# New places for row sums, loads and second-MLP units in an attention-plus-MLP kernel on one core

## The chip, the core and the metric

One core of one Trainium2 chip. The metric is the device time of one execution in microseconds, the median of several; less is better. A time from the timed runs is some 1.8 us longer than the span of the profile of the same execution, and I keep the two apart.

## The reference

```python
# q, k, v: (8, 12, 448, 64) fp32; w_in (768, 2048), w_out (2048, 768)
q_n, k_n = rmsnorm(q, g_q), rmsnorm(k, g_k)          # over the last dim
scores = q_n @ k_n.T / 8
attn = softmax(scores)
x = (attn @ v) -> (3584, 768)
h = x @ w_in
g = maximum(h, 0) + alpha * minimum(h, 0)            # alpha per column, 0 to 0.3
out = g @ w_out                                      # (3584, 768) fp32
```

## The kernel before

A *group* y is four heads of one batch (24 groups, three to a batch). Its q and k are loaded, squared, summed by row, turned into 1/rms (the *root*, two small ACT instructions), scaled, transposed by TensorE and copied out of PSUM as qT and kT. The score tiles follow two at a time; I call what is emitted between two pairs of them a *stretch* (index n). A stretch may hold the denominators ("dn"), the values ("av") or the transposes ("tps") of a group, and in it stand units of the MLP of an earlier batch: u (first MLP, 6 matmuls) and D (second MLP, 16 matmuls). `square`, `reduce`, `root` and `scale` prepare a group:

```python
    def square(y, nm):
        src = nat[y, nm].rearrange("p h j d -> p (h j d)")
        sq = ld.tile([128, 2 * J, D], FP32, name="sq", tag="sq", bufs=2)
        sqf = sq.rearrange("p n d -> p (n d)")
        if y < 2:
            nc.scalar.activation(out=sqf, in_=src, func=AF.Square)
        else:
            nc.gpsimd.tensor_mul(out=sqf, in0=src, in1=src)
        sqs[y, nm] = sq

    def reduce(y, nm):
        if nm == "q":
            ss_t[y] = ld.tile([128, 2, 2, J], FP32, name="ss", tag="ss", bufs=4)
        nc.vector.tensor_reduce(
            out=ss_t[y][:, "qk".index(nm)].rearrange("p h j -> p (h j)").unsqueeze(2),
            in_=sqs[y, nm], axis=AXIS_X, op=ALU.add,
        )
# ... root: two ACT instructions on ss -> rr; scale: tensor_mul by rr on POOL, for three tiles on DVE
    def turn(y):

        ps = psa.tile([128, 2, 512], FP32, name="tps", tag="acc")
# ...  14 transposes into ps, then on DVE:
        for tp, nm in zip(tps, "qk"):
            t = att.tile([128, 2, J, 64], FP16, name=f"{nm}T", tag=f"{nm}T", bufs=3)
            o = t.rearrange("p g j c -> p j g c")
            i4 = tp.rearrange("p j (g c) -> p j g c", g=2)
            if nm == "q":
                nc.vector.tensor_copy(out=o, in_=i4)
            else:
                nc.vector.tensor_scalar(
                    out=o, in0=i4, scalar1=gain[:, 0:1], scalar2=None, op0=ALU.mult
                )
            qkT[y, nm] = t
```

The two kinds of units share two PSUM buffers (tag "mm"). A first-MLP unit's result leaves PSUM by an ACT copy and a DVE max, a second-MLP unit's by a DVE copy:

```python
    def up(b, ft):
        x = xT[b].rearrange("p g i c -> p (g i) c")
        hT = psf.tile([128, 512], FP32, name="hT", tag="mm")
        for c in range(KM):
            nc.tensor.matmul(
                out=hT[:, :S],
                lhsT=w_in_sb[:, c, ts(ft, 128)],
                rhs=x[:, c, :],
                start=(c == 0),
                stop=(c == KM - 1),
            )
        ah = ffn.tile([128, S], FP16, name="ah", tag="ah", bufs=3)
        nc.scalar.activation(out=ah, in_=hT[:, :S], func=AF.Copy, scale=alpha_sb[:, ft : ft + 1])
        nc.vector.tensor_max(out=gT[:, ft, ds((b & 1) * S, S)], in0=hT[:, :S], in1=ah)

    def down(b0, t, oh):

        op = psf.tile([128, 512], FP32, name="op", tag="mm")
        for ft in range(NF):
            nc.tensor.matmul(
                out=op[:, :OH],
                lhsT=gT[:, ft, ts(t, 128)],
                rhs=w_out_sb[:, ft, ds(oh * OH, OH)],
                start=(ft == 0),
                stop=(ft == NF - 1),
            )
        if oh == 0:
            osb[b0, t] = ffn.tile([128, DM], FP32, name="osb", tag="osb", bufs=3)
        o = osb[b0, t]
        nc.vector.tensor_copy(out=o[:, ds(oh * OH, OH)], in_=op[:, :OH])
        if oh == 1:
            for half in range(2):
                bb, j = divmod(2 * t + half, J)
                nc.sync.dma_start(out=out4[b0 + bb, j], in_=o[ds(64 * half, 64)])
```

Where things are emitted, and the loop (cut):

```python
    for y in range(G, NG):
        n = J * y / 2
        at(n - 12, load_qk, y)
        for nm in "qk":
            at(n - 6, square, y, nm)
            after(n - 5, reduce, y, nm)
        after(n - 4, root, y)
        for nm in "qk":
            at(n - 3, scale, y, nm)
    for b in range(1, B):
        at(J * G * b / 2 - 4, load_v, b)
    turns = {J * y // 2 - 1: y for y in range(1, NG)}
# ... merge() spreads the carried D evenly among a batch's 16 u; half of the new D stay in the period
    after(0, root, 1)
    for nm in "qk":
        after(0, scale, 1, nm)
        after(1, reduce, 2, nm)
    after(2, root, 2)
    for nm in "qk":
        after(2, scale, 2, nm)

    for n in range(NB + 2):
        for f, a in prep.get(n, ()):
            f(*a)
        tiles = [divmod(m, J) for m in (2 * n, 2 * n + 1) if m < NG * J]
        for t in tiles:
            score(*t)
        late = []
        if n in dens:
            den(dens[n])
        if n in avs:
            attv(avs[n])
        plain = n not in dens and n not in avs and n not in turns
        wait = plain and gaps[n] and gaps[n][0][0] is up
        for t in tiles[:1] if wait else tiles:
            soft(*t)
        if wait:
            late = [(soft, t) for t in tiles[1:]]
        if n in dens:
            log(dens[n])
            late = [(invert, (dens[n],))]
        if n in turns:
            turn(turns[n])
        for f, a in gaps[n]:
            f(*a)
            if f is up and late:
                for g, c in late:
                    g(*c)
                late = []
        for g, c in late:
            g(*c)
        if n < first:
            spin(1 if not plain else 4)
        for f, a in post.get(n, ()):
            f(*a)
    for f, a in rest:
        f(*a)

```

The softmax here doesn't subtract the row's maximum and nothing guards it: scores larger than these inputs give would overflow.

## Time and profile before

| | before |
|---|---|
| timed runs | 490.51 us median (489.69 to 491.06, 4 runs) |
| profiled run | 488.3 us, span 486.5 us |
| first MLP unit starts | 51.92 us |
| listed waits of TensorE, 53 to 434 us | 15.5 us for DVE's max, 0.8 for DVE's multiply |

The profiled run is faster than each of the four timed ones. The lines of this profile are shown in the prediction below: the busy line, the table by stages, the waits of TensorE, the timeline of one large wait, and the start.

From the matmul records I took the start of each unit minus the start of the unit before it, and subtracted the smallest such difference of the same pair of kinds in this profile, for every kernel the same (1.133 us from u to u, 1.225 from u to scores, 2.597 from D to u, 0.505 from scores to transposes, and so on). The sum from the first u to the end is what TensorE lost; I call it *start-to-start loss*. Before: 24.55 us. The listed 0.25 is a loss of 0.41 in this measure, 1.02 is 1.18, 1.36 is 1.52: the list counts from the modelled end of the unit before, and that end lies some 0.16 us after the moment at which the next unit can start (a u is shown 1.29 to 1.30 long and followed by the next after 1.133).

### The profile page before, as it was taken

How to read it: one execution, taken by the hardware profiler on the slowest of the kernel's cores; microseconds unless marked ns; L12 is line 12 of the kernel's file. 1: busy time of each engine (PE TensorE's matmuls, PEld its weight loads, DVE VectorE, ACT ScalarE, POOL GpSimd, SP SyncE). 2: the span in 40 equal slices, each digit the busy share in tenths (PEclk: the TensorE clock that was granted, in tenths of full speed). 3: DMA queues.
4: the chain of work that ended last, by engine and by line, in shares of the span. 5: the costliest groups of instructions: out<-in, count | busy, mean ns of one | idle time of the engine just before them, and what ended most of it. 6: DMA issues, size and time to landing. Idle time of an engine off the chain costs nothing.

```text
span 486.5 us, 9510 instructions
## 1 busy us (share of the span) xinstructions
PE 448.4 (92%) x4072; PEld 234.3 (48%) x4072; DVE 216.7 (45%) x312; ACT 290.7 (60%) x399; POOL 166.7 (34%) x123
## 2 busy tenths in 40 slices
PE   6768799999999899999999899999999899999995
PEld 2334354544555444554555454554555454454563
DVE  1753545453552454544562444634643542334421
ACT  2688788666754667557765656666776475523300
POOL 2767574606504425405415244423435020000000
PEclk9599999999999999999999999999999999999999
DMA  7999996343605081333532280333511110120122
GB/s 210 158 248 244 239 197 117 71 109 87 134 23 124 20 165 51 91 98 85 96 74 74 70 166 5 105 80 97 100 34 34 34 34 0 34 66 0 34 65 66
DMA packets 32187, 45.46 MB, mean 93 GB/s; under 512 B 5008, under 2 KB 28560, under 8 KB 32144
## 3 DMA queue, kind: packets, MB, share of 16 engines
q1 hardware_dynamic: 19504, 31.67, 25.5%
q0 software_dynamic: 11776, 11.80, 15.3%
q10 hardware_dynamic: 864, 1.38, 1.0%
q8 instruction: 32, 0.52, 0.4%
q14 instruction: 11, 0.09, 0.1%
HBM read 45.62 MB, written 11.01 MB: 116 GB/s over the span
## 4 chain that ended last, share of the span: by engine, by line
PE 71%; DVE 13%; ACT 11%; DMA 2%; issue 2%; POOL 0%; DVEq 0%
PE op L266 31%; PE hT L249 20%; PE sc L189 6%; PE dn L212 6%; DVE ss L133 5%; DVE gT L258 5%; ACT ah L257 5%; PE av L212 5%; ACT expT L201 4%; PE tps L166 3%; DMA nat<-in_q_dram 2%; ACT rden L232 1%; DVE kT L176 1%; DVE qT L174 1%; ACT rden L227 1%
## 5 line engine op out<-in xcount | busy, mean ns | idle before, releaser
L201 ACT ACTIVATE expT<-sc,expb 128x896 f16<-128x896 f32 x168 | 160.2, 1003 | 48.7 <-PE sc L189 48.4
L249 PE MATMUL hT<-xT,w_in_sb 128*128 128x448 f16 x768 | 159.5, 352 | 17.9 <-DVE gT L258 17.0
L266 PE MATMUL op<-w_out_sb,gT 128*128 128x384 f16 x896 | 152.9, 326 | 0.2 <-DVE gT L258 0.2
L150 POOL TENSOR_TENSOR qs<-nat,rr 128x896 f16<-128x896 f32 x45 | 75.0, 1686 | 221.6 <-ACT rr L145 211.8
L257 ACT ACTIVATE ah<-hT,alpha_sb 128x448 f16<-128x448 f32 x128 | 81.1, 634 | 101.7 <-PE hT L249 100.7
L258 DVE TENSOR_TENSOR gT<-hT,ah 128x448 f16<-128x448 f32 x128 | 79.5, 624 | 104.3 <-ACT ah L257 104.2
L249 PEld LDWEIGHTS <-w_in_sb 128*128 128x128 f16 x768 | 72.3, 97 | 95.0 <-issue 35.4
L266 PEld LDWEIGHTS <-gT 128*128 128x128 f16 x896 | 85.0, 98 | 64.1 <-issue 10.5
L276 DVE COPY osb<-op 128x384 f32<-128x384 f32 x56 | 31.2, 558 | 112.1 <-PE op L266 112.1
L127 POOL TENSOR_TENSOR sq<-nat 128x896 f32<-128x896 f32 x44 | 72.9, 1676 | 3.0 <-DVE ss L133 3.0
L189 PE MATMUL sc<-qT,kT 64*64 64x448 f16 x672 | 50.2, 367 | 7.5 <-DVE kT L176 5.8
L133 DVE TENSOR_REDUCE ss<-sq 128x14 f32<-128x896 f32 x48 | 49.7, 1076 | 9.1 <-ACT sq L125 9.1
L240 DVE TENSOR_TENSOR xT<-av,rden 128x896 f16<-128x896 f32 x24 | 26.2, 1091 | 31.6 <-PE av L212 31.6
L212 PE MATMUL av<-expT,vt 64*64 64x448 f16 x672 | 36.0, 349 | 1.2 <-ACT rden L227 1.2
L212 PE MATMUL dn<-expT,ones 64*64 64x448 f16 x672 | 35.9, 349 | 0.0
L189 PEld LDWEIGHTS <-kT 64*64 64x64 f16 x672 | 13.4, 105 | 38.6 <-issue 30.2
L166 PE MATMUL tps<-ident,qs 128*128 128x128 f16 x336 | 24.0, 224 | 4.7 <-POOL qs L150 4.4
L212 PEld LDWEIGHTS <-vt 64*64 64x64 f16 x672 | 20.0, 107 | 13.5 <-issue 2.3
L166 PEld LDWEIGHTS <-qs 128*128 128x128 f16 x336 | 19.4, 100 | 13.5 <-issue 7.0
L212 PEld LDWEIGHTS <-ones 64*64 64x64 f16 x672 | 19.9, 107 | 11.8 <-issue 0.3
L227 ACT ACTIVATE rden<-dn 128x896 f32<-128x896 f32 x24 | 22.0, 916 | 4.8 <-PE dn L212 4.8
L232 ACT ACTIVATE rden<-rden 128x896 f32<-128x896 f32 x24 | 22.7, 947 | 0.3
(25 smaller groups left out, 97.3 us busy)
## 6 DMA issues: line engine op xcount, KB each, us to landing
out_dram<-osb SPq DMA_DIRECT2D x56, 192.0 KB, 2.7
nat<-in_q_dram SPq DMA_DIRECT2D x45, 224.0 KB, 3.8
nat<-in_k_dram SPq DMA_DIRECT2D x45, 224.0 KB, 5.0
vt<-in_v_dram POOLq DMA_DIRECT2D x16, 336.0 KB, 6.5
w_in_sb<-in_moe_w_in_dram POOLq DMA_DIRECT2D x4, 768.0 KB, 19.4
w_out_sb<-in_moe_w_out_dram POOLq DMA_DIRECT2D x4, 768.0 KB, 14.6
nat<-in_q_dram ACTq DMA_DIRECT2D x3, 224.0 KB, 6.9
nat<-in_k_dram ACTq DMA_DIRECT2D x3, 224.0 KB, 5.9
```

Of the source, the lines that this page charges most:

```text
L127: nc.gpsimd.tensor_mul(out=sqf, in0=src, in1=src)
L133: nc.vector.tensor_reduce(out=ss_t[y][:, "qk".index(nm)].rearrange("p h j -> p (h j)").unsqueeze(2), in_=sqs[y, nm], axis=AXIS_X, op=ALU.add,)
L150: eng.tensor_mul(out=t.rearrange("p j h d -> p h j d"), in0=nat[y, nm], in1=rr_t[y][:, "qk".index(nm)].unsqueeze(3).broadcast_to((128, 2, ...
L166: nc.tensor.transpose(tp[:, j, :], qs[y, nm][:, j].rearrange("p h d -> p (h d)"), ident)
L189: nc.tensor.matmul(out=sc[ds(64 * g, 64), par, :S], lhsT=kT[ds(64 * par, 64), g, j, :], rhs=qT[ds(64 * par, 64), g].rearrange("p j c -> p ...
L201: nc.scalar.activation(out=expT[y][:, j], in_=scs[y, j][:, :, :S], func=AF.Exp, scale=QK_SCALE, bias=expb[:, 0:1],)
L212: nc.tensor.matmul(out=acc[ds(64 * par, 64), g, :S], lhsT=weights(g, par, j), rhs=e[ds(64 * g, 64), j, par, :], start=(j == 0), stop=(j == ...
L249: nc.tensor.matmul(out=hT[:, :S], lhsT=w_in_sb[:, c, ts(ft, 128)], rhs=x[:, c, :], start=(c == 0), stop=(c == KM - 1),)
L257: nc.scalar.activation(out=ah, in_=hT[:, :S], func=AF.Copy, scale=alpha_sb[:, ft : ft + 1])
L258: nc.vector.tensor_max(out=gT[:, ft, ds((b & 1) * S, S)], in0=hT[:, :S], in1=ah)
L266: nc.tensor.matmul(out=op[:, :OH], lhsT=gT[:, ft, ts(t, 128)], rhs=w_out_sb[:, ft, ds(oh * OH, OH)], start=(ft == 0), stop=(ft == NF - 1),)
L276: nc.vector.tensor_copy(out=o[:, ds(oh * OH, OH)], in_=op[:, :OH])
```

## The change

It is meant to take the row sums out of DVE's way: they are to run while TensorE works on a D, and a D is to stand first wherever DVE has a multiply or copies to do. The start is to be shorter too: two loads less on ACT's queue, group 2's sums behind group 1's copies. The core of the diff:

```diff
@@ load_qk
-                (nc.scalar if y < G and g else nc.sync).dma_start(
+                (nc.scalar if y < 2 and g else nc.sync).dma_start(
@@ down: after its matmuls, before its copy
+        for f, a in jobs:
+            f(*a)
@@ where groups are prepared
+    turn_at = [J * y // 2 - 1 for y in range(NG)]
     for y in range(G, NG):
-        n = J * y / 2
-        at(n - 12, load_qk, y)
+        n = turn_at[y - 1] if y < G + 2 else last(y - G) + 2
+        at(n - 8, load_qk, y)
         for nm in "qk":
-            at(n - 6, square, y, nm)
-            after(n - 5, reduce, y, nm)
-        after(n - 4, root, y)
-        for nm in "qk":
-            at(n - 3, scale, y, nm)
+            at(n - 2, square, y, nm)
+            if y < G + 2:
+                after(n, reduce, y, nm)
+            else:
+                jobs.setdefault(n, []).append((reduce, (y, nm)))
+        roots[n + 1] = y
@@ distribution of the units
-        tail = len(new) if b == B - 1 else len(new) // 2
+        tail = len(new) if b == B - 1 else 2 + odd
...
+            free = n in avs or n in turns
+            while ups or old or new:
+                if old and (free or not ups):
+                    u = old.pop(0)      # a carried D first
+                elif ups:
+                    u = ups.pop(0)
+                else:
+                    u = new.pop(0)
...
@@ start
-    spin(32)
+    spin(34)
-        after(1, reduce, 2, nm)
-    after(2, root, 2)
-    for nm in "qk":
-        after(2, scale, 2, nm)
+        after(2, reduce, 2, nm)
+    roots[3] = 2
@@ loop: ahead of turn()
+        if n in roots:
+            y = roots[n]
+            root(y)
+            for nm in "qk":
+                scale(y, nm)
...
         for f, a in gaps[n]:
-            f(*a)
+            if f is down:
+                down(*a, jobs.pop(n, ()))
+            else:
+                f(*a)
...
-        for f, a in post.get(n, ()):
+        for f, a in jobs.pop(n, []) + post.get(n, []):
             f(*a)
```

Where a stretch with values has no D, the last lines emit its sums at the stretch's end. Cut here: in a stretch with denominators the second ACT step of the reciprocal now follows the second u, not the first; the last batch gets a carried D ahead of every third u.

More of the change, by code (lines that the diff above doesn't have):

```diff
@@ L260, with down @@
     osb = {}
-    def down(b0, t, oh):
+    def down(b0, t, oh, jobs=()):
         op = psf.tile([128, 512], FP32, name="op", tag="mm")
@@ L300 @@
     avs = {last(y) + 2: y for y in range(NG)}
-    prep, post = {}, {}
+    prep, post, roots = {}, {}, {}
     def at(n, f, *a):
@@ L307, in after @@
         post.setdefault(max(int(n), 0), []).append((f, a))
+    turn_at = [J * y // 2 - 1 for y in range(NG)]
+    turns = {n: y for y, n in enumerate(turn_at) if y}
+    jobs = {}
     for y in range(G, NG):
-        n = J * y / 2
-        at(n - 12, load_qk, y)
+        n = turn_at[y - 1] if y < G + 2 else last(y - G) + 2
+        at(n - 8, load_qk, y)
         for nm in "qk":
-            at(n - 6, square, y, nm)
-            after(n - 5, reduce, y, nm)
-        after(n - 4, root, y)
-        for nm in "qk":
-            at(n - 3, scale, y, nm)
+            at(n - 2, square, y, nm)
[4 more added lines that the diff above has]
+        roots[n + 1] = y
     for b in range(1, B):
         at(J * G * b / 2 - 4, load_v, b)
-    turns = {J * y // 2 - 1: y for y in range(1, NG)}
     UP, DOWN = 1.13, 2.6
-    def merge(ups, downs):
-        res, done = [], 0
-        for n, u in enumerate(ups):
-            while done < len(downs) and done * len(ups) <= n * len(downs):
-                res.append(downs[done])
-                done += 1
-            res.append(u)
-        return res + downs[done:]
     periods, carry = [], []
@@ L341 @@
         ]
-        tail = len(new) if b == B - 1 else len(new) // 2
-        periods.append(merge(ups, carry) + new[:tail])
+        tail = len(new) if b == B - 1 else 2 + odd
+        periods.append((ups, carry, new[:tail]))
         carry = new[tail:]
@@ L353 @@
         hi = last(G * b + 2 * G - 1) + 2
-        mlp = sum(u[0] for u in periods[b])
+        ups, old, new = (list(u) for u in periods[b])
+        mlp = sum(u[0] for u in ups + old + new)
         per = (mlp + sum(cost(n) for n in range(lo, hi))) / (hi - lo)
-        n, clock, done = lo, cost(lo), 0.0
-        for u in periods[b]:
-            while n < hi - 1 and clock + 0.5 * u[0] > per * (n - lo + 1):
-                n += 1
-                clock += cost(n)
-            gaps[n].append(u[1:])
-            clock += u[0]
-    rest = [u[1:] for u in periods[B - 1]]
+        clock = 0.0
+        for n in range(lo, hi):
+            clock += cost(n)
+            free = n in avs or n in turns
[6 more added lines that the diff above has]
+                    u = new.pop(0)
+                gaps[n].append(u[1:])
+                clock += u[0]
+                free = False
+                ahead = 0.5 * (UP if ups else DOWN)
+                if n < hi - 1 and clock + ahead > per * (n - lo + 1):
+                    break
+    ups, old, new = periods[B - 1]
+    rest = []
+    for n, u in enumerate(ups):
+        if n % 3 == 0 and old:
+            rest.append(old.pop(0)[1:])
+        rest.append(u[1:])
+    rest += [u[1:] for u in old + new]
     load_qk(0)
@@ L406 @@
             score(*t)
-        late = []
         if n in dens:
@@ L413 @@
         wait = plain and gaps[n] and gaps[n][0][0] is up
+        late = []
         for t in tiles[:1] if wait else tiles:
@@ L416 @@
         if wait:
-            late = [(soft, t) for t in tiles[1:]]
+            late = [(1, soft, t) for t in tiles[1:]]
         if n in dens:
             log(dens[n])
-            late = [(invert, (dens[n],))]
+            late = [(2, invert, (dens[n],))]
+        if n in roots:
[3 more added lines that the diff above has]
+                scale(y, nm)
         if n in turns:
             turn(turns[n])
+        done = 0
         for f, a in gaps[n]:
-            f(*a)
-            if f is up and late:
-                for g, c in late:
-                    g(*c)
-                late = []
-        for g, c in late:
+            if f is down:
+                down(*a, jobs.pop(n, ()))
+            else:
+                f(*a)
+                done += 1
+                if late and done == late[0][0]:
+                    for _, g, c in late:
+                        g(*c)
+                    late = []
+        for _, g, c in late:
             g(*c)
         if n < first:
-            spin(1 if not plain else 4)
-        for f, a in post.get(n, ()):
+            spin(4 if plain else 1)
+        for f, a in jobs.pop(n, []) + post.get(n, []):
             f(*a)
```

## The prediction

> **What bounds the kernel now.** I read first the page's busy line.
>
> ```profile
> PE 448.4 (92%) x4072; PEld 234.3 (48%) x4072; DVE 216.7 (45%) x312; ACT 290.7 (60%) x399; POOL 166.7 (34%) x123
> ```
>
> TensorE is the tight engine, so only what makes it stand can be won: 486.5 - 448.4 = 38 us, dummy matmuls ("spin") counted as busy. Where these 38 us lie I read from the busy table by stages.
>
> ```profile
> 0.00:53.25 53.25, 37.68 (x387) 17.96 (x388) 23.42 (x29) 37.33 (x49) 33.94 (x35) 0.90 1.03 214
> 53.25:160.00 106.75, 102.52 (x989) 53.60 (x988) 52.63 (x76) 73.20 (x101) 45.00 (x31) 1.00 0.55 119
> 160.00:268.00 108.00, 103.44 (x971) 54.42 (x970) 50.50 (x73) 68.76 (x96) 42.22 (x28) 1.00 0.37 84
> 434.00:486.50 52.50, 45.64 (x259) 24.97 (x256) 16.13 (x27) 10.13 (x16) 0.00 (x0) 1.00 0.18 46
> ```
>
> Columns: window, its length, busy us of PE, weight loads, DVE, ACT, POOL, then PE's clock, DMA share and GB/s. There are three stages. To 53 us only batch 0's attention runs; PE has spare time and the chain through ACT, DVE and POOL sets the pace. From 53 to 434 us attention alternates with MLP units and PE stands about 4%. In the tail only MLP is left. The list of waits, limited to 53 to 434 us and to PE, is short:
>
> ```profile
> PE hT L249 <- DVE gT L258: 15.5, 24, 1.4
> PE hT L249 <- DVE xT L240: 0.8, 1, 0.8
> ```
>
> So in 381 us there is one kind of wait: a first-MLP unit (I write u: 6 matmuls, 1.13 us) waits until DVE's max has emptied the PSUM buffer of the unit two before it. The timeline shows the two sizes of that wait:
>
> ```profile
> 216.34 1.30 PE L249 MATMUL hT<-xT,w_in_sb 128*128 128x448 f16 x6 [0.25 <-DVE gT L258]
> ...
> 218.88 2.07 DVE L133 TENSOR_REDUCE ss<-sq 128x14 f32<-128x896 f32 x2
> 219.42 0.63 ACT L257 ACTIVATE ah<-hT,alpha_sb 128x448 f16<-128x448 f32 x1 [0.21 <-PE hT L249]
> ...
> 220.87 1.26 DVE L258 TENSOR_TENSOR gT<-hT,ah 128x448 f16<-128x448 f32 x2
> 221.53 1.29 PE L249 MATMUL hT<-xT,w_in_sb 128*128 128x448 f16 x6 [1.02 <-DVE gT L258]
> ```
>
> The small one (0.25) is a third u in a row: a unit's ACT copy (0.63) and DVE max (0.62) with hand-overs free the buffer some 1.4 us after the unit, longer than the next unit's 1.13. The large one (1.02) is a pair of row sums, 2.07 us, in front of the max: the ACT copy was done at 220.05, the max began at 220.87.
>
> At the start I read the timeline:
>
> ```profile
> 4.96 0.60 ACTq L93 DMA_DIRECT2D nat<-in_q_dram  x1
> 8.68 0.60 ACTq L93 DMA_DIRECT2D nat<-in_k_dram  x1
> 9.33 1.79 ACT L125 ACTIVATE sq<-nat 128x896 f32<-128x896 f32 x2 [5.88 <-DMA nat<-in_k_dram]
> 12.07 1.69 POOL L150 TENSOR_TENSOR qs<-nat,rr 128x896 f16<-128x896 f32 x1 [8.37 <-DMA nat<-in_q_dram]
> ```
>
> ACT issues six loads, and the last two (group 2) stand ahead of its first square. They start only at 4.96 and 8.68 us. SP's fifth issue starts at 4.15 and the first chain step shown, a load, lasts from 0.74 to 4.13, so I read these late issues as waits for an earlier load to land: q of group 0 complete at 4.95, k at 8.67. The first square could run from about 5 us and the second from about 8.7; both wait to 9.33. The scale at 12.07 follows the root's end at 11.99; the load named beside it is, I think, a coincidence.
>
> [...]the max above starts after the row sums although its inputs were ready 0.8 us earlier. So emission order is the lever here.[...]PE stood from 9.38 to 13.82 us and the clock by windows went 0.96 (10 to 12 us), 0.50 (12 to 22), 0.98 (22 to 24).[...]
>
> **The change part by part.** The matmuls are the same except two more spins at the start. How the program's order differs I took from comparing both instruction orders, written by stretches between pairs of score tiles. D is a second-MLP unit (16 matmuls, 2.60), "av" the values (1.43), "dn" the denominators, "tps" a transpose (0.80).
>
> *Start.* Without the two late issues ACT squares q as soon as it lands, and k from about 8.7 to 9.7 instead of to 11.12. The root of q then starts at 9.7 rather than 11.44; row sum of k 9.75 to 10.8, its root to 11.4, its DVE scale (1.70) to 13.15 against 14.71: -1.6 us, working with the durations of the trace. The spins now last to 9.38 + 2 x 0.19 = 9.76, and the transposes come at about 12.1, so PE stands 2.3 instead of 4.4 us. If this keeps the clock up, the half-clock stretch goes: the k transposes win 0.47, the first scores 0.3 and the score rounds up to 22 us about 0.3, some 1 us. I give that 40%[...]: -0.4. The row sums of group 2 move behind the copies of group 1 (scores of group 1 about 1.2 us earlier), but ACT then waits for the root of group 2 before its next exponentials, so I keep 0.1. For group 3 likewise the copies come earlier and the root costs ACT its 0.55 elsewhere: 0. Sum of the start: -2.1 us.
>
> *Stalls of the steady stage, before.* Two batches repeat in about 108 us. Their stalls: 0.25, 1.02, 0.34, 0.25, 1.36, 0.34, 1.02 = 4.58. Three such rounds make 13.7; the first batch adds 1.36 + 1.02, less what the last round lacks: about the 15.5 of the list.
>
> *Stalls after.* A round now reads: tps D u | uuuu | dn uu | av D u | tps D | dn uuu | av uuu | tps uu | DD | dn D | av D u | tps D u | dn uuu | av D | tps D u | uuuuu | dn uuu | av D | tps uu D | dn D | av D. Where av comes with D, DVE does the multiply (1.09), the two sums (2.07) and D's copy by 3.8 us after the values' end; the next transposes end at 2.6 + 0.5 + 0.8 = 3.9. These sums cost nothing. What is left are runs of u: uuuu 0.45 (0.25 at the third, about 0.2 at the fourth because exponentials share ACT), uuuuu 0.55, "dn uuu" three times 0.3, "av uuu" 0.3, "tps uu D" 0.25: 2.45 us.
>
> One place gets worse. In "av uuu | tps uu" there is no D, so the sums fall to the end of the stretch. DVE then has: last max done 1.4 us after the last u, sums to 3.4, copies of qT and kT (1.25) to 4.65. PE has 0.5 of scores, 0.8 of transposes, 2.26 of uu and wants the new kT at 3.6: it stands about 1.1. The root now sits in that stretch ahead of the units' ACT copies and also waits for the sums, so the D after it finds its buffer 0.25 late. Together 1.35, once a round. A round thus costs 2.45 + 1.35 = 3.8 against 4.58: -0.8, and -2.4 for three. The last round is milder in the old kernel as in the new.
>
> *First batch.* It has no D to use until its end. "av uu | tps uu" occurs twice and "av u | tps D" once, all with the sums at the end: about 1.1, 1.1 + 0.25 + 0.3 and 0.85 = 3.6, against 1.36 + 1.02 = 2.4 before: +1.2.
>
> *Tail.* One D more is carried into it, which is only moved work. Runs of 5 to 6 u stall 6 x 0.25 now; three runs of 3 and one of 7 stall 3 x 0.25 + 3 x 0.25: 0.
>
> Sum: -2.1 - 2.4 + 1.2 = -3.3 us; 490.0 - 3.3 = 486.7.
>
> **Rivals.** (1) *The intended result is reached in full*: all large stalls go, kT is never late. The three stalls over 1 us of each round and the two of the first batch, eleven in all, lie 0.8 to 1.1 above an ordinary 0.25; without them 11 x 0.9 = 10 us go, with the start 12: 478. For it: the sums do lie inside D nearly everywhere. Against it: the new order has stretches without D, and runs of four and five u. (2) *The new kT wait eats everything*: if the root's wait in ACT also delays exponentials of the next scores, each of the six bad places costs 2 instead of 1.2 us, and the time is 490 to 491.[...] Against: ACT is only 60% busy and the exponentials of that stretch stand ahead of the root. (3) *The earlier start is swallowed* by the loads: the DMA share is near 1 up to 53 us and the first u needs w_in. Then only the steady part stays, about 489. Against: in the start no wait on w_in or on group 3's loads is listed, and w_in was issued at 21.3 us with 19.4 us to landing, some 8 us before it is needed.
>
> **Range and chances.** The start may give 1 to 3.5, the steady stage anything from +1 to -4 against my -1.2. I take 483.0 to 489.6. Over 2% would be 9.8 us, more than half of all listed PE stalls (15.5 + 1.5 in the tail) and the start together; I give it 0.05. Slower by 2% has nothing that speaks for it: 0.01.
>
> **What would show it.** Right: ACT's first square at about 5 us and the first transposes near 12.1; in 53 to 434 us the wait of hT for gT falls from 15.5 to about 8.5, and a new line appears, scores waiting for DVE's kT, about 6 us in some six places, one after each stretch of values without D; no row sum right before a max that PE waits for. Wrong if the kT line is missing (then rival 1), if the values' multiply or the osb copy becomes a releaser, or if the first u does not come about 2 us earlier than 51.9.

Marked cuts took out statements about the hardware that no trace or run of this case shows, and a reason in the second rival. The sum came to -3.3 us, and the start's -2.1 in it is -1.6 - 0.4 - 0.1. The -0.4 is an estimate, 40% of about 1 us, which I worked out from the transposes (0.94 us for seven) and scores that this profile shows at a clock of 0.50; that TensorE would keep its clock by standing 2.3 instead of 4.4 us was a guess. Whether the sums (1076 ns each in the profile) could be shortened was not tested.

## The result and the profile after

| | before | after |
|---|---|---|
| timed runs | 490.51 us (489.69 to 491.06) | 482.62 us (481.81 to 482.88) |
| span of the profile | 486.5 | 480.6 |
| first MLP unit | 51.92 | 49.39 |
| start-to-start loss from there on | 24.55 | 21.19 |

The ratio is 0.9838 (95% interval 0.9817 to 0.9858): 1.6% faster. A ratio is the mean time of one kernel's runs over the mean of the other's of the same rounds, so not quite the ratio of the medians. A control later, the changed kernel again on another chip job, gave 482.96 against 489.34 us, ratio 0.9867: the gain is 6.4 to 7.9 us depending on the session. The two ratios' intervals overlap (0.9847 to 0.9886 for the control). The prediction was 486.7 with 489.6 to 483.0 as its range; the result lies 0.4 us outside, on the fast side.

The busy line of the page after:

```profile
PE 451.2 (94%) x4074; PEld 234.9 (49%) x4074; DVE 217.3 (45%) x312; ACT 289.1 (60%) x399; POOL 167.0 (35%) x123
```

The busy table by stages of the changed kernel, columns as before (window, length, busy of PE, weight loads, DVE, ACT, POOL, then PE's clock, DMA share, GB/s):

```profile
0.00:50.72 50.72, 38.81 (x389) 17.88 (x390) 23.42 (x29) 37.05 (x49) 34.77 (x35) 0.93 1.11 220
50.72:157.50 106.78, 102.81 (x987) 53.85 (x987) 54.70 (x78) 73.43 (x103) 49.12 (x34) 1.00 0.54 121
157.50:265.50 108.00, 105.03 (x989) 54.96 (x988) 51.46 (x74) 69.67 (x96) 40.73 (x28) 1.00 0.38 88
428.00:480.60 52.60, 45.98 (x263) 25.45 (x261) 16.14 (x27) 9.57 (x16) 0.00 (x0) 0.97 0.18 46
```

The start is 2.5 us shorter between the two profiles, the tail is as it was. In equal windows of 108 us TensorE is busy 105.0 instead of 103.4 us (the windows hold slightly different work, so this is a direction and not a measure). The list of TensorE's waits from 53 to 428 us:

```profile
PE hT L249 <- DVE gT L258: 5.0, 19, 0.3
PE sc L189 <- ACT ah L257: 2.9, 5, 0.8
PE op L266 <- DVE gT L258: 1.7, 6, 0.3
PE sc L189 <- DVE kT L176: 0.4, 1, 0.4
```

No wait for a max is longer than 0.3 us any more; they are runs of u. New are six waits of scores. One of them, in the timeline, behind a stretch of values without a D:

```profile
132.88 0.62 DVE L258 TENSOR_TENSOR gT<-hT,ah 128x448 f16<-128x448 f32 x1 [0.92 <-ACT ah L257]
...
133.42 2.07 DVE L133 TENSOR_REDUCE ss<-sq 128x14 f32<-128x896 f32 x2
135.41 0.61 DVE L174 COPY qT<-tps 128x896 f16<-128x896 f16 x1
...
135.94 0.68 DVE L176 TENSOR_SCALAR kT<-tps,gain 128x896 f16<-128x896 f16 x1
136.01 1.14 ACT L257 ACTIVATE ah<-hT,alpha_sb 128x448 f16<-128x448 f32 x2
...
136.67 0.38 PE L189 MATMUL sc<-qT,kT 64*64 64x448 f16 x4 [0.52 <-ACT ah L257]
137.04 1.90 ACT L201 ACTIVATE expT<-sc,expb 128x896 f16<-128x896 f32 x2
137.33 1.95 PE L266 MATMUL op<-w_out_sb,gT 128*128 128x384 f16 x11 [0.28 <-DVE gT L258]
```

The list names ACT, but kT's copy ends at 135.94 + 0.68 = 136.62 and the scores start at 136.67: they waited for kT, which waited for the two sums. Only the second tile of the pair belongs to the new group here, so the first one still ran before the wait. The start after:

```profile
5.12 0.95 ACT L125 ACTIVATE sq<-nat 128x896 f32<-128x896 f32 x1 [1.69 <-DMA nat<-in_q_dram]
...
8.38 0.95 ACT L125 ACTIVATE sq<-nat 128x896 f32<-128x896 f32 x1 [2.31 <-DMA nat<-in_k_dram]
...
9.85 1.69 POOL L150 TENSOR_TENSOR qs<-nat,rr 128x896 f16<-128x896 f32 x1 [6.14 <-ACT rr L145]
...
11.60 0.56 PE L166 MATMUL tps<-ident,qs 128*128 128x128 f16 x7 [1.05 <-POOL qs L150]
```

Both squares now start as their load lands, where they waited until 9.33 us.

### The profile page after: what moved, and what is told of

Its sections match the earlier page's. It is cut to its first block, busy times and chain, and to the rows that moved or that the text cites. A ratio compares the mean times of both kernels' runs of the same rounds, so it can differ in the third digit from the quotient of the medians. Undisturbed runs are those within 1.5% of the kernel's fastest.

```text
span 480.6 us, 9494 instructions
## 1 busy us (share of the span) xinstructions
PE 451.2 (94%) x4074; PEld 234.9 (49%) x4074; DVE 217.3 (45%) x312; ACT 289.1 (60%) x399; POOL 167.0 (35%) x123
## 4 chain that ended last, share of the span: by engine, by line
PE 70%; ACT 12%; DVE 9%; issue 4%; POOL 3%; DMA 1%; SPq 0%; POOLq 0%; DVEq 0%; ACTq 0%
PE op L266 30%; PE hT L249 20%; ACT ah L257 6%; PE sc L189 6%; PE av L212 6%; PE dn L212 4%; DVE gT L258 4%; ACT expT L201 4%; DVE ss L133 3%; PE tps L166 2%; DMA nat<-in_k_dram 1%; POOL qs L150 1%; POOL sq L127 1%; ACT rden L227 1%; PE spin L289 1%
## 5 line engine op out<-in xcount | busy, mean ns | idle before, releaser
L189 PE MATMUL sc<-qT,kT 64*64 64x448 f16 x672 | 51.7, 370 | 9.9 <-DVE kT L176 4.5
L133 DVE TENSOR_REDUCE ss<-sq 128x14 f32<-128x896 f32 x48 | 49.8, 1076 | 7.0 <-ACT sq L125 7.0
```

The lines of the kernel that those rows point to most:

```text
L133: nc.vector.tensor_reduce(out=ss_t[y][:, "qk".index(nm)].rearrange("p h j -> p (h j)").unsqueeze(2), in_=sqs[y, nm], axis=AXIS_X, op=ALU.add,)
L189: nc.tensor.matmul(out=sc[ds(64 * g, 64), par, :S], lhsT=kT[ds(64 * par, 64), g, j, :], rhs=qT[ds(64 * par, 64), g].rearrange("p j c -> p ...
```

## The experiments

Fifteen kernels ran; all were correct. "b_" kernels are edits of the kernel before, "a_" kernels of the changed one. Where I compare kernels of different sessions I use the ratio to the kernel before in the same rounds. Where an expectation has a marked cut, a reason about the clock that no run shows was taken out; its figures stand. The question after the result was double: why the steady stage gained 3.4 us and not 1.2, and why the timed runs show 7.9 us (later 6.4) where the two profiles show 5.9.

**b_copy: the kernel before, unchanged.**

> The kernel before, unchanged, for a second profile. In the pair of profiles that I have the changed kernel is 5.9 us shorter (486.5 to 480.6), in the timed runs 7.9 us (490.5 to 482.6), and the profiled run of the kernel before took 488.3 us while its timed runs took 489.7 to 491.1. Theory: the first profile caught a lucky start, and this one shows a span of 488 to 489.5 with the first unit of the MLP 1.5 to 3 us later than 51.9 us, by a longer stretch at half the TensorE clock, and the stage from there on as before. Rival: the start is the same and the steady stage is 2 us longer, or the profile of before was simply a shorter run in all its parts.

Measured: 488.45 us, span of the profile 487.7, ratio 0.9983 (0.9959 to 1.0007). Loss from the first u on 24.58, as in the first profile; the first u at 53.04 instead of 51.92. The theory holds in kind: the later start is there, the rest is as before. In size it was too large, as both the span and the delay of 1.1 us lie below its ranges. The half-clock stretch of the first profile (11.85 to 22.09 us, granted clock 0.50) has a second one behind it here, in the middle of these three stretches:

```profile
22.91:26.32 3.41, 1.39 (x23) 0.88 (x21) 3.31 (x5) 2.62 (x5) 2.02 (x3) 1.00 1.06 145
26.32:29.73 3.41, 3.41 (x24) 1.24 (x28) 0.00 (x0) 1.98 (x3) 3.41 (x3) 0.50 1.12 237
29.73:33.14 3.41, 3.18 (x61) 1.65 (x53) 0.00 (x0) 3.33 (x5) 3.41 (x4) 1.00 1.15 271
```

In the stretch before it TensorE is busy 1.39 of 3.41 us, because group 1's scores wait 2.0 us for copies that stand behind group 2's sums. In the first profile the same instructions ran at a clock of 1.00, which these two stretches show:

```profile
22.09:25.50 3.41, 2.07 (x27) 1.08 (x27) 3.41 (x5) 2.09 (x3) 2.54 (x4) 1.00 0.96 144
25.50:28.92 3.42, 2.46 (x33) 1.29 (x37) 0.90 (x2) 3.11 (x5) 2.89 (x2) 1.00 1.13 216
```

So the profile that I predicted from was a lucky one by 1.1 us.

**b_early: only the two loads.**

```diff
-                (nc.scalar if y < G and g else nc.sync).dma_start(
+                (nc.scalar if y < 2 and g else nc.sync).dma_start(
```

> The kernel before with only the loads of group 2 moved off the ACT queue. Theory: ACT's first square starts at about 5.1 us and all that follows shifts by 2.0 to 2.5 us, so the first MLP unit comes at 49.5 to 50 us and the time is 2 to 2.5 us under the kernel before (ratio 0.995 to 0.996), the steady stage unchanged at 15.5 us of listed waits of hT. Rival: the shift is swallowed before the first MLP unit, by the order of the row sums of group 2 or by loads: under 1 us (ratio over 0.998).

Measured: 487.56 us (485.88 to 488.89), ratio 0.9960 (0.9933 to 0.9987); first square at 5.36, first u at 50.16 although this profile has a second half-clock stretch (24.23 to 27.64). The theory holds, the first u 0.2 us outside its range. The six runs fall in two heaps: 485.9 to 487.0 with a mean clock of 0.992 to 0.993, and 488.2 to 488.9 with 0.985 to 0.987.

**a_copy: the changed kernel again, as control.**

> The changed kernel again, as a control on the same chip as the next three, and for a second profile. Theory: 482 to 483 us, one stretch at half clock before 21 us and none after it; first MLP unit at 49.2 to 50.3 us, depending on when the k of group 0 lands (8.0 to 9.3 us in the profiles so far). Rival: a second half-clock stretch as in the second profile of the kernel before; then 484.

Measured: 482.96 us (482.51 to 483.23), ratio 0.9867 (0.9847 to 0.9886); first u at 49.76, loss 21.19 as in the first profile of this kernel. One half-clock stretch, 13.42 to 20.25 us, and none behind it. The theory holds; the ratios of the a_ kernels below are to be read against this one.

**a_issue: the changed kernel with the two loads back on ACT** (the same line, reversed).

> The changed kernel with the loads of group 2 back on the ACT queue. Theory: first square back at about 9.2 us, first transposes near 13.7, first unit of the MLP 1.7 to 2.2 us later than the 49.4 to 49.7 of the changed kernel: 484.3 to 485 us, steady stage unchanged. Rival: the start of the changed kernel comes mainly from the new order of group 2 and of the roots: under 1 us lost.

Measured: 484.73 us, ratio 0.9898 against the control's 0.9867: 1.5 us lost. First square at 8.58, first transposes at 13.07 (not 13.7), first u at 51.23 instead of 49.39 and 49.76 in the two profiles of the changed kernel; loss from there on 21.23, unchanged. The theory holds: the loads are worth 1.5 to 1.8 us.

**a_spin: more dummy matmuls at the start.**

```diff
-    spin(34)
+    spin(46)
```

> The changed kernel with 46 dummy matmuls instead of 34 before the first transposes, so that TensorE is busy up to them. Theory: the half-clock stretch from about 13 to 20 us is left out or shortened and the start is 0.8 to 1.5 us shorter than in the changed kernel: 481 to 482 us. Rival: [...]the score rounds are paced by ACT anyway: within 0.4 us of the changed kernel.

Measured: 482.73 us, ratio 0.9864, the control's 0.9867. The profile has no half-clock stretch at all in its first 480 us (mean granted clock 1.0), and the first u comes at 49.57, no earlier. The rival holds as to the time: the early half-clock stretch, 13.45 to 20.28 us in the changed kernel, was not worth filling this way. The longer dummies also held the first transposes to 12.35 us (11.60 without), so what full clock alone would give is not isolated.

**a_post: sums always at the end of the stretch.**

```diff
-                down(*a, jobs.pop(n, ()))
+                down(*a)
```

> The changed kernel, but with the row sums always at the end of the stretch instead of inside the second-MLP unit; the order of the MLP units is the new one. Theory (place of the sums is what counts): the transposes' copies come after the sums also behind values with a second-MLP unit, about 0.8 us lost in one such stretch and 1.1 in another of each round of two batches, about 2 us a round and 6 us in all: 488 to 489 us, ratio to the kernel before 0.995 to 0.998. Rival (the order of the MLP units is what counts): under 2 us lost against the changed kernel, ratio about 0.985 to 0.988.

Measured: 485.31 us, ratio 0.9914 (0.9892 to 0.9936), 2.6 us behind a_spin of the same session; loss 23.82 instead of 21.19, which is 2.6 us. TensorE's waits from 53 to 428 us:

```profile
PE hT L249 <- DVE gT L258: 5.0, 19, 0.3
PE sc L189 <- ACT ah L257: 2.9, 5, 0.8
PE op L266 <- DVE gT L258: 2.6, 6, 0.8
PE sc L189 <- DVE kT L176: 1.9, 4, 0.5
```

Two kinds of places got worse, as expected, by 0.57 and 0.46 start to start instead of 0.8 and 1.1 each. So the place inside D is worth 2.6 us. The theory (about 6 us) was far too large and the rival (under 2) too small.

**a_oldplan: the old distribution of the units in the changed kernel.**

```diff
-        tail = len(new) if b == B - 1 else 2 + odd
-        periods.append((ups, carry, new[:tail]))
+        tail = len(new) if b == B - 1 else len(new) // 2
+        periods.append(merge(ups, carry) + new[:tail])
 ... and the old loop that fills the stretches
```

> The changed kernel with the old distribution of the MLP units over the stretches; sums inside a second-MLP unit where the stretch with values has one, else at its end. Theory (the place of the sums is all that matters, in start-to-start losses of TensorE): the old round lost 5.97 us, of which the sums ahead of a max cost 1.11 + 0.77 + 0.77 more than an ordinary stall; they go, a late kT of about 0.6 comes once a round: about 3.9 us a round against 5.06 in the changed kernel, so 1 to 3 us faster than it, 479.5 to 481.5. Rival (second-MLP units first in stretches with values or transposes is what gained): 1 us or more slower than the changed kernel.

Measured: 481.92 us, ratio 0.9831 (0.9814 to 0.9848), control 0.9867; loss 20.10 against 21.19. The rival is refuted: with the sums in place, a D first in stretches with values or transposes is not what gained; the old distribution with the new places of the sums loses 20.10 us where the kernel before lost 24.55. The theory's size was too large: I had expected 3.5 us less loss and 1.1 came, because in the first batch, which has no D, the sums at the end of a stretch still cost 1.66 and 1.06, and single stalls were 0.5 to 0.67 rather than 0.41.

**a_den: sums behind the denominators where a stretch with values has no D.**

```diff
+            has = any(f is down for f, ... in gaps[n])
+            at(n - (2 if has else 3), square, y, nm)
+            if has: jobs.setdefault(n, []).append((reduce, (y, nm)))
+            else:   early.setdefault(n - 1, []).append((reduce, (y, nm)))
 ... loop, after den(dens[n])
+        for f, a in early.pop(n, ()):
+            f(*a)
```

> The changed kernel, but where a stretch with values has no second-MLP unit the sums go one stretch earlier, behind the denominators and ahead of the units there. Theory (the late kT behind such stretches is what is left to win): the losses of 1.06 once a round and of 0.9, 1.06, 0.17 and 0.49 in the first batch go, some 5 us less 0.5 given back: 477.5 to 478.5 us. Rival: the sums then stand ahead of the maxima of the stretch with denominators and cost as much there: within 1.5 us of the changed kernel.

Measured: 477.54 us (477.33 to 477.96), ratio 0.9746 (0.9729 to 0.9763), loss 15.75 instead of 21.19. The theory holds in place and size. The waits of TensorE from 53 to 425 us are down to this:

```profile
PE hT L249 <- DVE gT L258: 5.0, 19, 0.3
PE op L266 <- DVE gT L258: 0.9, 3, 0.3
```

The scores' line is gone, and TensorE waits no more than before for a max in the stretches with denominators: the sums run during the 1.43 us of the denominators and the first u. This version is faster than both kernels, by 2.5% and 1.2%.

**a_oldden: both of the last two.** The distribution of a_oldplan with the sums' places of a_den.

> The old distribution of the MLP units with the sums inside second-MLP units or behind the denominators: both experiments that did not lose, together. Theory: the old distribution has fewer runs of four and five first-MLP units, so with the late kT gone it loses about 3.4 us a round against 4.05 in a_den, 0.3 us less in the first batch or the same: losses 13.5 to 14.5 us, time 475.5 to 476.8. Rival: sums behind the denominators cost more where a second-MLP unit stands first there: 477.5 or more.

Measured: 478.76 us, ratio 0.9783, loss 17.05. It is slower than a_den, and the theory is refuted. A round of two batches loses about 3.7 us instead of 4.05, but the first batch still has a stall of 0.67 behind its first transposes (none in a_den), the stretches of the last batch lose 0.7 us more, and the tail 2.9 instead of 2.5 us in its longer runs of u. So once no sums stand in the way, the new distribution is the better one, and while they do, the old one is.

**a_r2: group 2's sums, root and scale at their old places.**

```diff
-        after(2, reduce, 2, nm)
-    roots[3] = 2
+        after(1, reduce, 2, nm)
+    after(2, root, 2)
+    for nm in "qk":
+        after(2, scale, 2, nm)
```

> The changed kernel, with only the row sums, root and scale of group 2 back at their old places (sums ahead of group 1's copies). Theory: the scores of group 1 come about 1.2 us later again, TensorE idles about 2 us near 24 us and in some of the runs the clock falls for a second window of 3.4 us; so the mean is 0.7 to 2 us over the changed kernel (483.3 to 484.6) and the runs spread by 2 us or more, where the changed kernel spread by 1.1. Rival (my prediction's reckoning): 0.1 us, no spread.

Measured: 484.06 us (483.71 to 484.55, 4 runs), ratio 0.9878, control 0.9867. The slowdown, about 0.5 by ratio and 1.1 by medians, is at or below the theory's low end, and the two ratios' intervals overlap; the spread of 2 us did not come, and the profile shows no second half-clock stretch. From the first scores to the first u it takes 35.39 instead of 34.97 us: 0.42 by order. Most of the rest I put down to the landing of group 0's k, without a test: ACT's second square starts between 7.84 and 9.25 us in the profiles in which it follows the landing, at 9.12 here against 8.38 in the first profile of the changed kernel.

**b_r2: the same moved into the kernel before** (nearly the reverse edit: root and scale follow stretch 3 instead of standing in it).

> The kernel before with only the row sums, root and scale of group 2 moved behind the copies of group 1. Theory: the scores of group 1 come 1.2 us earlier, TensorE no longer idles 2 us near 24 us, so the second half-clock stretch (26.3 to 29.7 us in the second profile of before) is gone; 0.4 us by order and 1.1 us by clock, ratio to before 0.9965 to 0.9975. Rival: the stretch comes or not[...]: ratio over 0.998 and the profile may show it.

Measured: 489.14 us, ratio 0.9992 (0.9975 to 1.0009). No gain. The profile shows why: group 1's scores are earlier, but the second half-clock stretch now lies at 36.55 to 39.96 us. The theory is refuted as to the stretch, and the ratio is the one that the rival gave.

**b_start: loads, 34 dummies and group 2 together, in the kernel before.**

> The kernel before with the whole of the new start (loads, 34 dummy matmuls, group 2) and nothing else. Theory: start and rest add up: 3.0 to 3.8 us under the kernel before, ratio 0.992 to 0.994, first MLP unit near 49.6 us, start-to-start losses of TensorE from there on 24.5 us as before. Rival: the two parts of the start overlap, ratio over 0.995.

Measured: 487.41 us, ratio 0.9956 (0.9940 to 0.9973); loss from the first u on 24.59, first u at 50.91. About 2 us instead of 3.0 to 3.8: the ratio is the rival's, whether or not for its reason. A half-clock stretch lies at 35.5 to 38.9 us, where group 3's sums stand ahead of group 2's copies.

**b_start3 and a_r3: group 3's sums behind group 2's copies, added to b_start, and taken back in the changed kernel.**

```diff
+        if y == 3:
+            for nm in "qk":
+                at(4, square, y, nm)
+                after(6, reduce, y, nm)     # a_r3: after(5, ...)
+            after(7, root, y)               # a_r3: after(6, ...)
+            for nm in "qk":
+                after(7, scale, y, nm)      # a_r3: at(7, ...)
+            continue
```

> The kernel before with the new start and also group 3's row sums, root and scale at their new places (sums behind group 2's copies). In b_start the stretch at half clock had not gone but moved to 35.5 to 38.9 us, where the sums of group 3 still stand ahead of the copies of group 2. Theory: with group 3 moved, TensorE no longer stands there, no half-clock stretch comes between 21 and 49 us, the first MLP unit comes at 49.4 to 50 us and the time is 0.9 to 1.3 us under b_start: 486.1 to 486.5 us. Rival: the later stretch [...]shows up elsewhere; then within 0.4 us of b_start.

> The changed kernel with only group 3's sums, root and scale back at their old places. Theory: TensorE stands about 2 us near 34 us again, and in most runs the clock is halved for 3.4 us there: 0.7 to 1.5 us over the changed kernel, 483.7 to 484.5 us. Rival (my prediction's reckoning, 0 for group 3): within 0.3 us of the changed kernel, 482.6 to 483.2.

Measured, a_r3: 483.79 us (483.63 to 484.62), ratio 0.9880, control 0.9867; the first u at 50.73 us, loss 21.13, and this in the table by windows:

```profile
32.38:35.79 3.41, 1.26 (x25) 0.66 (x26) 2.21 (x3) 1.65 (x4) 2.91 (x4) 1.00 1.15 275
35.79:39.20 3.41, 3.41 (x37) 1.40 (x33) 0.00 (x0) 2.89 (x4) 3.41 (x3) 0.50 1.22 235
```

About 0.6 us by ratio and 0.8 by medians, at the theory's low end; the two ratios' intervals overlap, but the profile has the forecast stretch. Measured, b_start3: 487.57 us, ratio 0.9953, no gain over b_start: the half-clock stretch had moved on to 44.3 us. That is the rival.

**b_start4: groups 2, 3 and 4 at their new places in the kernel before.**

```diff
-        if y == 3:
+        if y < 5:
+            m = 6 if y == 3 else 9
 ... square at m - 2, sums after m, root and scale after m + 1
```

> The kernel before with the new start and the new places of the squares, sums, roots and scales of groups 2, 3 and 4; from group 5 on, and for the MLP units, all is old. In b_start3 group 4's squares came late (its sums had to wait 0.44 us between q and k, its root held ACT for 1.06 us) and the half-clock stretch came at 44.3 to 47.7 us. Theory: [...]first MLP unit at 49.3 to 50 us, 1.0 to 1.4 us under b_start3: 486 to 486.5 us, ratio 0.992 to 0.993. Rival: the stretch comes[...] in the old kernel whatever the order; then still near 487.5 us, ratio 0.995.

Measured: 486.25 us (485.52 to 488.5), ratio 0.9956 (0.9934 to 0.9979); four runs at 485.5 to 486.4 with a clock of 0.995 to 0.999, two at 487.5 and 488.5 with 0.985. By the median the theory holds, by the ratio the rival. The profile still has a half-clock stretch at 43.4 to 46.8 us, so new places for groups 2 to 4 don't end it.

What the profiles show of the clock after 20 us is this. In b_copy TensorE was busy 1.39 of 3.41 us, in a_r3 1.26 of 3.41, in b_start4 1.86 of 3.41 (39.99 to 43.40), and each time some 3.41 us at a clock of 0.50 followed. In the control it was busy 1.81 of 3.41 us (30.49 to 33.90), in the first profile 2.07 of 3.41 (22.09 to 25.50), and the clock stayed at 1.00. Seven profiles have a half-clock stretch after 20 us: five (b_copy, b_early, b_r2, b_start, a_r3) after sums ahead of copies, two (b_start3, b_start4) where no sums stand ahead of copies. What decides whether the clock falls was not shown, and I take no rule from these cases.

Two things stay open. Added to the kernel before, the new start with groups 2 to 4 gave about 2.2 us by ratio (b_start4), not the 3.0 that the changed kernel's gain leaves for the start; the ratio's interval is some 1.1 us either way. And some parts were never run alone: the two more dummies, the later second step of the reciprocal, the later loads and squares from group 5 on, the new order of the last batch.

## Why the prediction was wrong, point by point

*The sum.* The step that failed is "Sum: -2.1 - 2.4 + 1.2 = -3.3 us" (counted from 490.0, the median of the three runs I then had). In the steady stage the mechanism was right (waits for a max go, a late kT comes) and the sizes were not. In the start the loads were right and the clock was misread. Each of the three terms was about 0.9 us too slow:

| term | predicted | measured | from |
|---|---|---|---|
| start | -2.1 | -3.0 | control's -6.4 less the -3.4 of the loss; -2.5 between the first two profiles, -3.7 against b_copy; a remainder, not measured by itself |
| three rounds | -2.4 | -3.3 | loss without first batch and tail: 18.0 to 14.7 |
| first batch | +1.2 | +0.3 | loss 3.65 to 3.99 |
| tail | 0 | -0.4 | 7 x 0.41 to 6 x 0.41 |

The first session's -7.9 is 1.5 us more than these terms; there the kernel before ran 490.5 us, in the later sessions 488.6 to 489.9. I can't assign that difference to an instruction.

*Rounds.* I added up the listed waits, 4.58 us a round. Start to start a round lost 5.97: each of its seven stalls counts 0.16 more than listed, and some 0.3 us lies in bits too small for the list. For the new round I reckoned 3.8 and 5.06 was lost. So the difference per round was nearly right for the two whole rounds (0.8 against 0.9 each), but by luck: the errors of 1.4 and 1.3 us cancel. In the new round the late kT cost 1.06 us, not 1.35, and the runs of u 3.75, not 2.45. What I counted as the third is half a round before them and half a round after, with the last batch in it; there the loss fell by 1.5 us (6.1 to 4.6), where I had put 0.8 and waved the rest away with "The last round is milder in the old kernel as in the new". That step failed: the stalls of the last half round fell from 3.1 to 1.6 us, those of the first half stayed at 2.5 and 2.6.

*First batch.* I had the late kT right in all its places: three here and one in each round, six in all, and all six are in the list, under two names. In the list they come to 3.3 us, where I had forecast about 6, and the wait of hT for gT to 5.0 (with op's 6.7), where I had forecast 8.5. I had its size wrong: 0.91, 1.06 and 0.49 + 0.17 start to start, not 1.1, 1.35 and 0.85, and the old stalls of the first batch were 2.70, not 2.4. a_den then showed that the wait was as real as predicted: taking it away gave 5.4 us.

*Start.* First square at 5.12 (predicted about 5), first transposes at 11.60 (12.1), first u 2.5 us earlier (about 2): the loads are right, and a_issue confirms 1.5 to 1.8.

The clock I had wrong twice. First, I gave 0.4 us to the guess that it stays up when TensorE stands 2.3 instead of 4.4 us. In the first profile the clock fell at 11.85 us, when TensorE had stood for 2.5 us (from 9.38), and in the changed kernel it fell at 13.45 although TensorE had not stood longer than 1.05 us at a time since its first dummy. And the early half-clock stretch is worth nothing that a_spin could find.

Second, for the orders of groups 2 and 3 I kept 0.1 and 0. Between the first two profiles that is right: from the first scores to the first u it takes 34.91 us before and 34.97 after, though group 1's scores come 1.2 us earlier, as predicted. It is wrong where a later half-clock stretch comes, which the one profile that I had did not show: 36.22 us in b_copy. Put back alone in the changed kernel, group 2 lengthens this part by 0.42 us without such a stretch and group 3 by 0.62 with one (35.59). In the kernel before, moving group 2 alone (b_r2) or group 3 after it (b_start3) gained nothing clear.

*Rivals.* The first, that the intended result is reached in full, was too optimistic: kT was late. Its estimate of 478 is close to the 477.5 of a_den, the kernel with that wait removed; it took 10 us for the stalls and 2 for the start, where 8.8 and some 3 came. It also counted eleven stalls over 1 us, and start to start there are ten. The second did not happen: the six places cost 0.91 + 1.06 + 0.66 + 3 x 1.06 = 5.8 us start to start, about 1 us each and not 2. The third is refuted by the first u at 49.4.

*The range.* It was built around the single profile. Its timed runs, 1.4 to 2.7 us slower than the profiled one, said before any experiment that the kernel has more than one length; b_copy showed that it is the start.

## What to carry to other kernels

Where an engine works in the order of the program (here a max of DVE, its ACT copy done at 220.05 us, began at 220.87, behind the sums), put long work that nobody waits for (here 2.07 us of sums) where the engines that wait have a long task of their own, and check every place where that task is missing: the late kT behind stretches without a D cost 5.4 us, more than the change gained in the rounds, and moving the sums one stretch earlier won it back. Measure losses from start to start, not by the listed idle time, when the profile's ends of an engine's work are modelled (here 0.25 us listed for a stalled u, 0.41 lost). Before predicting from one profile, compare its time with the timed runs: the start can have more than one length (here 51.92 and 53.04 us to the first u of one and the same kernel).
